# Reordering the 64 KB blocks of keys and values over the partitions in a single-token attention kernel

## The chip, the cores and the metric

The kernel runs on one core of one Trainium2 chip. The core has a matrix engine (PE, with a row of its own, PEld, for loading weights), a vector engine (DVE), a scalar engine (ACT), a general engine (POOL) and a sequencer that here only starts transfers (SP). 16 DMA engines move data between the chip's main memory and an on-chip memory of 128 partitions. The metric is the device time of one execution in microseconds (us). Before the change the median of three runs is 1275.43 us (1275.26 to 1275.6).

## The reference

One token goes through a layer norm, an attention over cached keys and values, and a small dense block; both have a residual.

```
H, Sk, Dh = 32, 32768, 128        # heads, cached positions, head size; D = 512, F = 1376
q = (layernorm(x) @ wq)                                      # one row of 32 x 128
scores = einsum("bhqd,bhkd->bhqk", q, k_cache) * Dh**-0.5
o = einsum("bhqk,bhkd->bhqd", softmax(scores), v_cache)
h = x + o @ wo
out = h + mish(layernorm(h) @ w1 + b1) @ w2
```

All tensors are bf16. The two caches have 32 heads of 32768 positions of 128 numbers each: 8 MB of keys and 8 MB of values a head, 537 MB in all. Each number is read once. The softmax and the weighted sum run over all positions of a head, in whatever order they stand, as long as keys and values stand in the same one.

## The kernel before

The on-chip memory holds a ring of six slots (`ring`), each of 32 KB a partition. A head's keys fill two slots, its values two: 64 KB a partition, 256 rows of 128 numbers (`SCOLS` = 256). Keys have two homes, for even and odd heads; values have one. `keys_of` (line 505) views a head's cache as `(p r) d -> p r d`: partition p takes the p-th of 128 blocks of 64 KB, that is positions 256 p to 256 p + 255. `tiles_of` (line 502) views the two slots in the same shape.

SP starts all large transfers, in the order written out in `order`: the query weights, keys of head 0, then for each head h from 1 on keys of h and values of h - 1, and at the end the output weights, the last values and the dense block's weights. The loop over `order` in `program` waits, before each transfer, for the work that frees its slots (`freed_by`, `done_with`; line 553), and then starts it (line 584 for keys and values). All go through `start`, so the profile names their issues, and the waits before them, by line 545. Most heads' keys and values come in one transfer of 8 MB each; the first keys, the last values and a few others are cut along r by `pieces`, so that work can begin or end on a part. Values of head h are started once the product of head h - 1 with its values is done; keys of head h once the keys of head h - 2 have been transposed.

For each head PE transposes the 256 tiles of 128 x 128 keys in groups of eight (line 685), DVE copies each group out of the accumulator (`ering`, line 691), and PE multiplies the group by the query, one column of scores a tile (line 661). DVE takes the maximum (line 725), two small matrix products spread it (lines 731 and 736), ACT takes the exponential of all scores with its sum (line 741), and PE multiplies the 256 tiles of values by the weights into one column (line 712). Column r of the scores and tile r of the values belong to the same positions, because keys and values are laid out alike. The product with the values of a head runs after the transposes of the next head's keys. PE and DVE run these rounds as loops; the head number is a register.

After the last head come the output projection, the second layer norm and the dense block, whose weights are loaded at the very end: `w1` in four transfers of 344 KB, `w2` in three transfers of 128 partitions and one of the last 96 rows (line 545 again in the profile).

Of the kernel before, what the change touches and what calls it, by code (L numbers as in the profile page):

```python
# [307 lines left out]
def build_kernel(nc, A_x, A_k_cache, A_v_cache, A_wq, A_wo, B_w1, B_b1, B_w2, out):  # L308
# [16 lines left out]
    SCOLS = HALVES * TPS  # L325
# [103 lines left out]
    def pieces(what):  # L429
        kind, h = what  # L430
        if what in (("k", 0), ("v", H - 1)):
            at = CUTS[kind]
        else:
            at = [TPS] if what in (("k", 1), ("v", 1)) else [64] if what == ("k", H - 1) else []
        return list(zip([0] + at, at + [SCOLS]))
# [4 lines left out]
    def uncut(what):  # L440


        kind, h = what
        for r in CUTS[kind]:
            if not cut_at(kind, h, r) and (h == 0 or cut_at(kind, h - 1, r)):
                n = 1
                while h + n < H and not cut_at(kind, h + n, r):
                    n += 1
                yield r, n

    def later_k(h):

        if h == 2:
            for r in CUTS["k"]:
                yield r, sum(1 for n in range(1, H) if n == 1 or not cut_at("k", n, r))
# [17 lines left out]
    def slot_of(what):  # L473
        if what in HOMES:
            return HOMES[what]
        if what[0] in ("w1", "w2"):
            return HOMES[WL]
        return V_HOME if what[0] == "v" else what[1] % 2 * HALVES
# [14 lines left out]
    def freed_by(what):  # L493
        if what == WO:
            return done_with("k", H - 2, 0, SCOLS)
        if what[0] == "k" and what[1] > 1:
            return done_with("k", what[1] - 2, 0, SCOLS)
        if what == ("v", 0):
            return [free_name(WQ)]
        return []  # L500

    def tiles_of(what):
        return ring[:, slot_of(what):slot_of(what) + HALVES, :].rearrange("p s (r d) -> p (s r) d", d=Dh)

    def keys_of(cache, h):
        return cache[0, h, :, :].rearrange("(p r) d -> p r d", r=SCOLS)

    wq_v = ring[:, slot_of(("wq",)), :].rearrange("p (k n) -> p k n", k=KC)
    wo_v = ring[:, slot_of(("wo",)), :].rearrange("p (j n) -> p j n", j=32)
# [6 lines left out]
    def done_with(kind, h, r0, r1):  # L516
        if kind == "v":
            return [f"pv{h}_{r1}" if r1 in V_EVENTS else f"pv{h}"]
        return [free_name(("k", h, half)) for half in range(HALVES) if r0 < (half + 1) * TPS and r1 > half * TPS]
# [15 lines left out]
    def program(S):  # L535
# [8 lines left out]
        def start(dst, src, s):  # L544
            S.dma(SP, lambda: sp.dma_start(dst, src).then_inc(s, 16))  # L545
# [3 lines left out]
        for what in order:  # L549
            slot = slot_of(what)  # L550
            if what == ("k", 1):
                S.stay(SP)
            S.wait(SP, freed_by(what))
            flat = ring[:, slot, :]
            if what[0] == "wq":
                S.wait(SP, ["b1z"])
                start(b1r[0:FJ // 2, :], B_b1[0:FJ * 128].rearrange("(i p) -> i p", i=FJ // 2), s_b1)
                start(b1r[FJ // 2:FJ // 2 + 1, 0:FLAST], B_b1[FJ * 128:F].rearrange("(o p) -> o p", o=1), s_b1)
            elif what[0] == "wo":
                start(flat, A_wo.rearrange("(p j) n -> p (j n)", j=32), ready[slot])  # L560
            elif what == WL:
                start(wol_v, A_wo[(H - 1) * Dh:H * Dh, :], s_wl)
            elif what[0] == "w1":
                k = what[1]
                start(w1_v[:, k, :], B_w1[k * 128:(k + 1) * 128, :], w1_sems[k])
            elif what[0] == "w2":
                n = what[1]
                if n + 1 < len(W2_J):
                    j0, j1 = W2_J[n], W2_J[n + 1]
                    start(w2_v[:, j0:j1, :].rearrange("p (i s) n -> p i (s n)", s=2),  # L570
                          B_w2[j0 * 128:j1 * 128, :].rearrange("(i p s) n -> p i (s n)", p=128, s=2), w2_sems[n])
                else:
                    start(w2_v[0:FLAST, FJ, :], B_w2[FJ * 128:F, :], w2_sems[n])
            else:
                kind, h = what
                rows = keys_of(A_k_cache if kind == "k" else A_v_cache, h)
                for r0, r1 in pieces(what):
                    if kind == "v" and h:
                        S.wait(SP, done_with(kind, h - 1, r0, r1))
                    if what == ("k", 1):  # L580
                        s = ready[slot] if r0 else s_k1
                    else:
                        s = cut_sems[kind][r0] if r0 else ready[slot]
                    start(tiles_of(what)[:, r0:r1, :], rows[:, r0:r1, :], s)


                for r, n in uncut(what) if kind == "v" else later_k(h):
                    S.dma(SP, lambda r=r, n=n: sp.sem_inc(cut_sems[kind][r], 16 * n))
# [277 lines left out]
    log = {}  # L866
    counted = _Sched(nc, False, events, sems, log)
    program(counted)
    nc.sync.dma_start(ring[:, slot_of(WQ), :], A_wq.rearrange("(p k) n -> p (k n)", k=KC)).then_inc(ready[slot_of(WQ)], 16)
    with nc.Block() as block:  # L870
        for eng_name, attr in ((POOL, "gpsimd"), (SP, "sync"), (DVE, "vector"), (ACT, "scalar"), (PE, "tensor")):
            emitter = _Sched(nc, True, events, sems, log, only=eng_name)

            def _run(eng, emitter=emitter):
                program(emitter)
            getattr(block, attr)(_run)
            assert emitter.cnt == counted.cnt
# [31 lines left out]
```

## Time and profile before

| what | value |
|---|---|
| median of the runs | 1275.43 us |
| span of the profiled execution | 1273.6 us |
| from the span to the median | 1.8 us |
| PE busy | 1016.5 us (80%) |
| DVE busy | 715.8 us (56%) |
| bytes moved | 548.35 MB, 431 GB/s over the span |
| packets of 8 KB or more | 12350 - 2998 = 9352 |
| PE's longest wait in total | 204.9 us, 30 times, for keys (line 685) |

The span goes from the first to the last instruction of one execution taken by the hardware profiler. A window row gives, for a stretch of that span, the busy time of each engine with its instructions in brackets, the granted clock of PE as a share, the mean busy share of the 16 DMA engines and what they moved in GB/s. In some windows the share comes out slightly above 1. The chain of waits is followed back from the last instruction: at each step to what released it. A transfer's line gives its size, the number of such transfers, and the median time from issue to landing.

### The profile page before, as it was taken

How to read it: one execution, taken by the hardware profiler on the slowest of the kernel's cores; microseconds unless marked ns; L12 is line 12 of the kernel's file. 1: busy time of each engine (PE TensorE's matmuls, PEld its weight loads, DVE VectorE, ACT ScalarE, POOL GpSimd, SP SyncE). 2: the span in 40 equal slices, each digit the busy share in tenths (PEclk: the TensorE clock that was granted, in tenths of full speed). 3: DMA queues.
4: the chain of work that ended last, by engine and by line, in shares of the span. 5: the costliest groups of instructions: out<-in, count | busy, mean ns of one | idle time of the engine just before them, and what ended most of it. 6: DMA issues, size and time to landing. Idle time of an engine off the chain costs nothing.

```text
span 1273.6 us, 54445 instructions
## 1 busy us (share of the span) xinstructions
PE 1016.5 (80%) x25046; PEld 988.9 (78%) x25046; DVE 715.8 (56%) x1252; ACT 20.6 (2%) x71; POOL 0.9 (0%) x8
## 2 busy tenths in 40 slices
PE   4689877779777789777788777797777897777995
PEld 4689877779777789777788777797777887777994
DVE  2566664456654466644466644566544666445661
ACT  0000000000000000000000000000000000000000
POOL 0000000000000000000000000000000000000000
PEclk9888876778877688867788776787777887677885
DMA  9999999999999999999999999999999999999998
GB/s 403 445 417 437 432 438 434 440 428 428 432 438 430 445 428 428 430 440 428 445 430 428 430 438 430 440 434 428 428 438 432 434 440 428 428 436 434 426 435 353
DMA packets 12350, 548.35 MB, mean 431 GB/s; under 512 B 1360, under 2 KB 1590, under 8 KB 2998
## 3 DMA queue, kind: packets, MB, share of 16 engines
q1 hardware_dynamic: 12340, 548.22, 99.7%
q8 instruction: 8, 0.13, 0.0%
q10 hardware_dynamic: 2, 0.00, 0.0%
HBM read 548.21 MB, written 0.00 MB: 430 GB/s over the span
## 4 chain that ended last, share of the span: by engine, by line
DMA 54%; DVE 23%; PE 18%; issue 2%; SPq 2%; POOL 0%; POOLq 0%
DMA ring<-in_A_k_cache_dram 51%; DVE ering L691 23%; PE ops L712 9%; PE tps L685 6%; DMA ring<-in_A_v_cache_dram 2%; SPq L545 2%; PE sps L661 1%; DMA ring<-in_B_w_dram 1%; PE hlp L736 1%; PE hlp L731 1%; PE hlp L746 0%; PE tps L854 0%; DVE pmax L725 0%; DVE perm L859 0%; DVE gmax L733 0%
## 5 line engine op out<-in xcount | busy, mean ns | idle before, releaser
L685 PE MATMUL tps<-identb,ring 128*128 128x128 bf16 x8192 | 668.3, 232 | 209.4 <-DMA ring<-in_A_k_cache_dram 204.9
L691 DVE COPY ering<-tps 128x1024 bf16<-128x1024 bf16 x1024 | 669.4, 692 | 259.7 <-PE tps L685 258.5
L685 PEld LDWEIGHTS tps<-identb,ring 128*128 x8192 | 522.2, 104 | 212.2 <-issue 212.2
L661 PE MATMUL sps<-qcur,ering 128*128 128x1 bf16 x8192 | 343.7, 164 | 7.7 <-DVE ering L691 6.7
L661 PEld LDWEIGHTS sps<-qcur,ering 128*128 128x128 bf16 x8192 | 309.2, 97 | 10.7 <-DVE ering L691 9.4
L712 PEld LDWEIGHTS ops<-pbuf,ring 128*128 128x128 bf16 x8192 | 226.3, 103 | 24.4 <-issue 15.1
L712 PE MATMUL ops<-pbuf,ring 128*128 128x1 bf16 x8192 | 231.3, 165 | 10.8 <-DMA ring<-in_A_v_cache_dram 8.3
L720 DVE TENSOR_TENSOR oT<-ops,rtotc 128x1 f32 x31 | 5.0, 162 | 109.8 <-PE ops L712 109.8
L733 DVE TENSOR_REDUCE gmax<-hlp 1x1 f32<-1x128 f32 x32 | 8.9, 278 | 67.5 <-PE hlp L731 67.5
L738 DVE TENSOR_SCALAR nbias<-hlp 128x1 f32<-128x1 f32 x32 | 5.1, 158 | 63.4 <-PE hlp L736 63.4
L741 ACT ACTIVATE pbuf<-sps,nbias 128x256 bf16<-128x256 f32 x32 | 15.2, 474 | 1219.9 <-PE ops L712 1166.7
L731 PE MATMUL hlp<-ident,pmax 128*1 128x128 f32 x64 | 17.9, 379 | 5.2 <-issue 5.2
L725 DVE TENSOR_REDUCE pmax<-sps 128x1 f32<-128x256 f32 x32 | 13.6, 425 | 14.3 <-PE sps L661 14.3
L736 PE MATMUL hlp<-gmax,onesmat 1*128 1x1 f32 x64 | 18.5, 356 | 0.4 <-DVE gmax L733 0.4
L736 PEld LDWEIGHTS hlp<-gmax,onesmat 1*128 1x128 f32 x64 | 15.8, 304 | 1.3 <-DVE gmax L733 0.9
L746 PE MATMUL hlp<-esum,onesmat 128*128 128x1 f32 x64 | 12.1, 258 | 4.8 <-issue 1.0
L746 PEld LDWEIGHTS hlp<-esum,onesmat 128*128 128x128 f32 x64 | 9.5, 188 | 7.4 <-issue 7.4
L640 PE MATMUL hlp<-xnT,ring 128*128 128x1 bf16 x128 | 3.6, 165 | 9.2 <-DMA ring<-in_A_wq_dram 9.2
L640 PEld LDWEIGHTS hlp<-xnT,ring 128*128 128x128 bf16 x128 | 3.5, 104 | 9.3 <-issue 9.3
L720 DVE TENSOR_TENSOR oL<-ops,rtotc 128x1 bf16<-128x1 f32 x1 | 0.2, 161 | 14.3 <-PE ops L712 14.3
L731 PEld LDWEIGHTS hlp<-ident,pmax 128*1 128x1 f32 x64 | 2.8, 81 | 5.8 <-issue 5.3
L748 DVE RECIPROCAL rtotc<-hlp 128x1 f32<-128x1 f32 x32 | 5.4, 168 | 2.7 <-PE hlp L746 1.4
(77 smaller groups left out, 40.1 us busy)
## 6 DMA issues: line engine op xcount, KB each, us to landing
ring<-in_A_k_cache_dram SPq DMA_DIRECT2D x3, 4096.0 KB, 40.2
ring<-in_A_v_cache_dram SPq DMA_DIRECT2D x3, 4096.0 KB, 15.3
ring<-in_A_k_cache_dram SPq DMA_DIRECT2D x3, 2048.0 KB, 30.5
ring<-in_A_k_cache_dram SPq DMA_DIRECT2D x1, 6144.0 KB, 44.6
ring<-in_A_wq_dram SPq DMA_DIRECT2D x1, 4096.0 KB, 12.2
ring<-in_A_wo_dram SPq DMA_DIRECT2D x1, 4096.0 KB, 35.6
ring<-in_A_v_cache_dram SPq DMA_DIRECT2D x1, 2048.0 KB, 16.1
ring<-in_B_w_dram SPq DMA_DIRECT2D x4, 344.0 KB, 20.7
```

The lines of the kernel that those rows point to most:

```text
L545: S.dma(SP, lambda: sp.dma_start(dst, src).then_inc(s, 16))
L640: S.step(PE, lambda h=h, kc=kc: t_.matmul(Q_REG[:, h:h + 1], wq_v[:, kc, h * Dh:(h + 1) * Dh], xnT[:, 0, kc:kc + 1], start=(kc == 0), stop ...
L661: S.step(PE, lambda r=r: t_.matmul(S_ps[:, col0 + r:col0 + r + 1], ering[:, bg % NE, r, :], qcur[:, :], start=True, stop=True), name=(name ...
L685: S.step(PE, lambda r=r, at=at: t_.matmul(tb[:, r * 128:(r + 1) * 128], key_tile(S, at), identb[:, :], is_transpose=True, start=True, stop ...
L691: S.step(DVE, lambda: v.tensor_copy(ering[:, bg % NE, :, :].rearrange("p r d -> p (r d)"), tb[:, :]), name=f"ev{bg}", waits=[f"trb{bg}"], ...
L712: S.step(PE, lambda r=r: t_.matmul(o_ps[:, 0:1], vt[:, r, :], pbuf[:, r:r + 1], start=(r == 0), stop=(r == SCOLS - 1)), name=(names or Non ...
L725: S.step(DVE, lambda: v.tensor_reduce(pmax[:, :], S_ps[:, 0:SCOLS], AXX, ALU.max), name=f"pmax{h}", waits=[f"qkh{h}"], kind="pmax")
L731: S.step(PE, lambda: t_.matmul(A_REG, pmax[:, :], ident[:, :], start=True, stop=True), name=f"A{h}", waits=[f"pmax{h}", "ident", f"rcp{h - ...
L733: S.step(DVE, lambda: v.tensor_reduce(gmax[:, :], A_REG, AXX, ALU.max), name=f"gmax{h}", waits=[f"A{h}"], kind="gmax")
L736: S.step(PE, lambda: t_.matmul(B_REG, onesm[0:1, :], gmax[:, :], start=True, stop=True), name=f"B{h}", waits=[f"gmax{h}", "consts0"] + ([] ...
L741: S.step(ACT, lambda: a.activation(pbuf[:, :], S_ps[:, 0:SCOLS], ACTF.Exp, bias=nb[:, :], scale=SC, accum_out=esum[:, :]), name=f"exp{h}", ...
L746: S.step(PE, lambda: t_.matmul(C_REG, onesm[:, :], esum[:, :], start=True, stop=True), name=f"C{h}", waits=[f"exp{h}"], kind="C")
```

## The change

Every load of keys and of values takes another order of the head's 64 KB blocks. Where partition 8 e + i (e from 0 to 15, i from 0 to 7) had block 8 e + i, it now has block 16 i + e. `keys_of` gives a view of four dimensions, (16, 8, 256, 128), and the start of a transfer folds the last two on the source's side, and the rows of the tile on the destination's: the source then counts 16 by 8 runs, the destination 128 partitions, each run as long as before. Cuts along r are as before.

```diff
     def keys_of(cache, h):
-        return cache[0, h, :, :].rearrange("(p r) d -> p r d", r=SCOLS)
+        return cache[0, h, :, :].rearrange("(i e r) d -> e i r d", e=16, r=SCOLS)
...
-                    start(tiles_of(what)[:, r0:r1, :], rows[:, r0:r1, :], s)
+                    start(tiles_of(what)[:, r0:r1, :].rearrange("p r d -> p (r d)"),
+                          rows[:, :, r0:r1, :].rearrange("e i r d -> e i (r d)"), s)
```

Keys and values go through the same function, so both are permuted alike.

## The prediction

> **What bounds the kernel now.** I read the page first, then the stages in windows, the chain of waits, the wait list of the SP queue, and last the end of the run in small windows. From the page: the engines' busy time, the share of the DMA engines by slice, the queue, and the chain that ended last.
>
> ```profile
> span 1273.6 us, 54445 instructions
> PE 1016.5 (80%) x25046; PEld 988.9 (78%) x25046; DVE 715.8 (56%) x1252; ACT 20.6 (2%) x71; POOL 0.9 (0%) x8
> DMA  9999999999999999999999999999999999999998
> DMA packets 12350, 548.35 MB, mean 431 GB/s; under 512 B 1360, under 2 KB 1590, under 8 KB 2998
> q1 hardware_dynamic: 12340, 548.22, 99.7%
> DMA 54%; DVE 23%; PE 18%; issue 2%; SPq 2%; POOL 0%; POOLq 0%
> ```
>
> One queue, filled by SP, carries all the bytes, and its packets take 99.7% of the time of 16 engines. No compute engine is full. The windows over five stages of the steady part say whether the rate wanders (columns: busy time of each engine, granted clock, DMA share, GB/s):
>
> ```profile
> core 0: us, PE busy (x) PEld busy (x) DVE busy (x) ACT busy (x) POOL busy (x), PEclk, DMA share, GB/s
> 200.00:400.00 200.00, 157.19 (x3911) 153.63 (x3907) 111.02 (x191) 3.39 (x12) 0.00 (x0) 0.76 1.01 435
> 400.00:600.00 200.00, 159.92 (x3926) 156.36 (x3927) 113.36 (x194) 2.83 (x10) 0.00 (x0) 0.76 1.00 432
> 600.00:800.00 200.00, 161.29 (x4023) 157.66 (x4020) 116.43 (x200) 2.83 (x10) 0.00 (x0) 0.77 1.00 433
> 800.00:1000.00 200.00, 163.23 (x4024) 159.80 (x4023) 117.24 (x200) 2.83 (x10) 0.00 (x0) 0.77 1.00 435
> 1000.00:1200.00 200.00, 163.15 (x4057) 159.75 (x4055) 117.68 (x203) 2.82 (x10) 0.00 (x0) 0.78 1.00 433
> ```
>
> 432 to 435 GB/s in every stage: the pace is that of a fixed link. Two rows of the chain of waits in order of time, each the first transposes after a head's keys have come, give it exactly, with the wait before the first of them and the two lines of loads of a whole head:
>
> ```profile
> 201.54 45.43 DMA ring<-in_A_k_cache_dram
> 247.37 3.59 PE tps L685 x32
> ...
> 1021.44 3.59 PE tps L685 x32
> ```
>
> ```profile
> ring<-in_A_v_cache_dram SPq DMA_DIRECT2D x30, 26.1
> ring<-in_A_k_cache_dram SPq DMA_DIRECT2D x29, 45.0
> ```
>
> Between them lie 774.07 us and 20 heads (the starts repeat every 77.4 us, for two heads): 38.70 us a head. A head is 8 MB of keys and 8 MB of values, 256 blocks of 64 KB, 16 for each engine if they share evenly: 2.42 us a block, 433.5 GB/s. The 32 heads are 32 x 38.70 = 1238 us of the 1273.6; the rest is the start, the weights and the end. A value load takes 26.1 us from issue to landing, and half of a head, 19.35 us, is its own transfer, so 6.7 us of other loads are still queued when it is issued.
>
> **The change part by part.** The arithmetic is untouched: keys and values are permuted alike, and neither the maximum, the sum nor the weighted sum over all positions asks for their order. Instructions on PE, DVE and ACT stay as they are. Bytes stay. The number and length of contiguous runs stay too: a partition still takes one whole 64 KB block of a head, or the same cut of it. Three things differ.
>
> (1) *SP's issues.* The source of each load gets one more dimension. The wait list of the SP queue and its timeline (rows of start, length, instruction):
>
> ```profile
> SPq L545 <- PE ops L712: 1165.8, 33, 38.8
> ```
>
> ```profile
> 1207.62 0.33 SPq L545 DMA_DIRECT2D ring<-in_A_v_cache_dram  x1
> 1208.05 0.38 SPq L545 DMA_DIRECT2D ring<-in_A_wo_dram  x1
> ```
>
> An issue holds SP for 0.33 to 0.38 us, and SP waits 1165.8 us for PE. Dearer issues vanish in that wait. Only the five pieces of the last head's values are issued with the end near; were each issue twice as long, 5 x 0.38 = 1.9 us would be the most. I take 0, bounds 0 to +1.9 us. Behind that wait stand the value load and the next key load; the 6.7 us of queue cover them.
>
> (2) *The order of reading.* Now an engine walks blocks 1 MB apart, and the 16 engines together walk 16 neighbouring blocks, where before each had neighbours of its own. A gain would need a pace above that of the fixed link: the best 200 us window has 435 for the 433.5 of the sum, and 1238 x (1 - 433.5/435) = 4.3 us is the most to be had. A loss: the slowest stretch of steady loading is early,
>
> ```profile
> 64.00:103.00 39.00, 35.32 (x882) 34.52 (x880) 26.22 (x45) 0.56 (x2) 0.00 (x0) 0.82 0.98 421
> ```
>
> 421 for 433.5, which over all heads would be 1238 x 0.030 = +37 us. Between -4.3 and +37 I take 0, by the five rows in which five different sets of heads give one rate.
>
> [...]
>
> (3) *How a load is divided among the engines.* This decides. Before, both sides count 128 rows. After, the source counts 16 times 8 and the destination 128, so an engine's sixteenth should be one value of e: partitions 8e to 8e + 7, walked in order. If that is not the share the engines had, two of them may now write into the same part of the on-chip memory at the same time, and the even pace rests on their not doing so. No load of the trace has unlike counts on its two sides. The nearest one is the only large one that isn't 128 rows, the last 96 rows of w2 (96 KB), at the very end:
>
> ```profile
> ring<-in_B_w_dram SPq DMA_DIRECT2D x1, 96.0 KB, 10.0
> ```
>
> ```profile
> 1267.50:1268.00 0.50, 0.50 (x9) 0.50 (x6) 0.22 (x1) 0.00 (x0) 0.00 (x0) 0.50 1.04 381
> 1268.00:1268.50 0.50, 0.38 (x2) 0.08 (x1) 0.18 (x3) 0.21 (x1) 0.00 (x0) 0.50 0.99 358
> 1268.50:1268.80 0.30, 0.00 (x0) 0.00 (x0) 0.27 (x2) 0.00 (x0) 0.00 (x0) 0.50 0.80 215
> 1268.80:1269.10 0.30, 0.00 (x0) 0.00 (x0) 0.27 (x2) 0.00 (x0) 0.20 (x1) 0.50 0.48 171
> 1269.40:1269.90 0.50, 0.50 (x16) 0.30 (x16) 0.00 (x0) 0.00 (x0) 0.00 (x0) 0.50 0.45 170
> ```
>
> Divide GB/s by the share: 366, 362, 269, 356, 378. For 0.3 us the busy engines move 0.74 of their bytes, and then recover: packets are stretched while loads divided in two ways overlap. What stretches them is not shown; two writers on one entry would do it. The last row says more: near 0.45 of the engines are still busy 1.4 us after the others (from 1268.5 to 1269.9), so engines lead one another by about 1.4 us at most.
>
> [...]
>
> The price, from rows: if no two engines meet, 0. If two always meet, each block takes 2 x 2.42 us, a head 77.4 us, and 32 heads 1238 us more. Compute doesn't limit then: PE's 163 us of 200 is 32 us a head. A lead helps: an engine that is 1.4 us ahead leaves the shared entry earlier. Four blocks are 9.68 us; met all the way they take 19.35, with the lead 19.35 - 1.4 = 17.95, a factor of 1.855. Between 1.855 and 2 I take 1.93. Of the two ends, nothing and twice, I take the upper: the row of stretched packets is the only one in which loads are divided in unlike ways. It is a choice on thin ground.
>
> *Sum.* The profiled execution: 1273.6 + 0 + 0 + 0.93 x 1238 = 2425 us. The median of the runs, 1275.4, is 1.8 us above the span, which I add: **2427 us**. With factors of 1.855 and 2, 2334 to 2514.
>
> **The rivals.**
>
> *No two engines meet, or the shares are what they were.* Then the fixed link goes on setting the pace: 1275.4, from 1273 to 1278. For it: five stages at one rate, whatever is loaded. Against it: the stretched row. This one ends on the other side, not slower, and it decides as soon as the 16 engines still write to 16 separate entries.
>
> *They meet, but drift apart.* [...] The lead now is 1.4 us; if it grows on the way, the loads end anywhere between 1 and 1.85 times as long. With the stretch of the row, 362/269 = 1.35, it is 1275.4 + 0.35 x 1238 = 1709 us. Against it: a load's end is its slowest engine's, and an engine that runs ahead soon waits for SP, which waits for PE, and starts level again.
>
> [...]
>
> *Neighbouring blocks read better:* at most -4.3 us, 1271 us. Against it: the DMA share is full and the rate flat, so reading is not what is waited for.
>
> That the change does nothing at all is out, since the addresses differ by construction.
>
> **How the numbers follow.** Two engines on one entry throughout (2334 to 2514): 0.45. Meeting and drifting (1310 to 2334): 0.17. Memory (1278 to 1312, and beyond by the page): 0.06. No difference: 0.24. Reading better: 0.08. A measurement of this kernel tells about 0.2%, 2.6 us, from no change. So slower 0.45 + 0.17 + 0.06 = 0.68, same 0.24, faster 0.08. The time is that of the likeliest, 2427 us, its own range 2334 to 2514. The range for 8 in 10 has to take in the no-difference case, since leaving it and the gain out would drop 0.32; it goes from 1272, most of the gain left out, to 2515, the full doubling.
>
> **What would show it.** In the changed profile: if right, the DMA share stays near 99% while GB/s falls to 220 to 235, a head takes 72 to 77 us, PE falls to some 45% busy, and value loads take over 45 us to land. SP's wait for PE must not be what grows first. A rate above 400 GB/s with the time within 3 us of before would make the third step wrong: the shares, or the entries, are not what limits. A rate between, changing along the run, would be drift. A small loss with an even rate would be the memory, and a gain of over 4.3 us would mean that the link is not fixed.

## The result and the profile after

The changed kernel takes 2610.63 us (median of six runs, 2603.67 to 2620.92), the kernel before 1275.39 us: a ratio of 2.0476, 95% interval 2.0448 to 2.0503. The profiled execution has a span of 2606.8 us and a time of 2608.6 us.

The lines of the page after the change that answer to those shown of before: engines, share of the DMA engines, packets, the queue.

```profile
span 2606.8 us, 54445 instructions
PE 1034.0 (40%) x25046; PEld 1003.8 (39%) x25046; DVE 716.6 (27%) x1252; ACT 20.6 (1%) x71; POOL 1.0 (0%) x8
DMA  9999999999999999999999999999999999999987
DMA packets 12350, 548.35 MB, mean 210 GB/s; under 512 B 1360, under 2 KB 1590, under 8 KB 2998
q1 hardware_dynamic: 12340, 548.22, 99.1%
```

The same instructions, the same 12350 packets, the same bytes, and still a busy share of 99.1% over all 16 engines: each packet lasts about twice as long (a 64 KB block 4.987 us on the mean, before 2.422). PE's busy time has hardly moved (1016.5 to 1034.0 us); only its share has fallen. That is the trap of a busy share: 99% is what a queue shows at 431 GB/s and at 210.

Windows of the steady part, with the columns of before (the last two are DMA share and GB/s):

```profile
400.00:800.00 400.00, 157.83 (x3870) 153.79 (x3870) 110.98 (x190) 2.83 (x10) 0.00 (x0) 0.63 1.00 211
1200.00:1600.00 400.00, 158.43 (x3870) 154.38 (x3870) 110.97 (x190) 2.83 (x10) 0.00 (x0) 0.63 1.00 211
2000.00:2400.00 400.00, 156.55 (x3870) 152.51 (x3870) 110.37 (x190) 2.82 (x10) 0.00 (x0) 0.63 1.01 212
```

An even 211 GB/s from end to end: no drift along the run. The chain of waits in order of time gives the pace; the rows are the wait for keys after a head's values have been used, 22 heads apart:

```profile
542.32 31.88 another core or an unknown queue
...
2306.24 31.84 another core or an unknown queue
```

The chain does not name what these waits are for ("an unknown queue"); the list of waits does. First the two lines of before, then those after:

```profile
PE tps L685 <- DMA ring<-in_A_k_cache_dram: 204.9, 30, 7.9
PE ops L712 <- DMA ring<-in_A_v_cache_dram: 8.3, 6, 4.0
```

```profile
PE tps L686 <- DMA ring<-in_A_k_cache_dram: 986.4, 34, 36.8
PE ops L713 <- DMA ring<-in_A_v_cache_dram: 530.7, 36, 29.2
```

1763.92 us for 22 heads are 80.18 us a head, where it was 38.70: a factor of 2.072. PE now waits for keys 986.4 us instead of 204.9, and for values 530.7 us instead of 8.3. The lines of the whole loads, from issue to landing:

```profile
ring<-in_A_v_cache_dram SPq DMA_DIRECT2D x30, 71.9
ring<-in_A_k_cache_dram SPq DMA_DIRECT2D x29, 111.4
```

71.9 us for a value load (26.1 before). Half a head is now 40.1 us, so 31.8 us of other loads are queued at the issue instead of 6.7: SP is further ahead than before, and is not what is late.

### The profile page after: what moved, and what is told of

Same layout as the page of the kernel before. It is cut to its first block, busy times and chain, and to the rows that moved or that the text cites. A ratio compares the mean times of both kernels' runs of the same rounds, so it can differ in the third digit from the quotient of the medians.

```text
span 2606.8 us, 54445 instructions
## 1 busy us (share of the span) xinstructions
PE 1034.0 (40%) x25046; PEld 1003.8 (39%) x25046; DVE 716.6 (27%) x1252; ACT 20.6 (1%) x71; POOL 1.0 (0%) x8
## 2 busy tenths in 40 slices
DMA packets 12350, 548.35 MB, mean 210 GB/s; under 512 B 1360, under 2 KB 1590, under 8 KB 2998
## 3 DMA queue, kind: packets, MB, share of 16 engines
q1 hardware_dynamic: 12340, 548.22, 99.1%
## 4 chain that ended last, share of the span: by engine, by line
another core or an unknown queue 56%; DVE 21%; PE 18%; DMA 3%; issue 2%; SPq 0%; POOL 0%; ACT 0%; POOLq 0%
DVE ering L692 21%; PE ops L713 9%; PE tps L686 6%; DMA ring<-in_A_k_cache_dram 2%; DMA ring<-in_B_w_dram 2%; PE sps L662 1%; PE hlp L732 1%; PE hlp L737 1%; PE hlp L747 0%; SPq L545 0%; PE tps L855 0%; PE sps L835 0%; DVE pmax L726 0%; DVE perm L860 0%
## 5 line engine op out<-in xcount | busy, mean ns | idle before, releaser
L686 PE MATMUL tps<-identb,ring 128*128 128x128 bf16 x8192 | 678.2, 234 | 990.7 <-DMA ring<-in_A_k_cache_dram 986.4
L686 PEld LDWEIGHTS tps<-identb,ring 128*128 x8192 | 530.0, 105 | 993.5 <-issue 993.5
L713 PE MATMUL ops<-pbuf,ring 128*128 128x1 bf16 x8192 | 234.1, 165 | 535.9 <-DMA ring<-in_A_v_cache_dram 530.7
L742 ACT ACTIVATION_READ_ACCUMULATOR pbuf<-sps,nbias 128x1 f32 x32 | 6.2, 193 | 0.0
```

Of the source, the lines that this page charges most:

```text
L686: S.step(PE, lambda r=r, at=at: t_.matmul(tb[:, r * 128:(r + 1) * 128], key_tile(S, at), identb[:, :], is_transpose=True, start=True, stop ...
L713: S.step(PE, lambda r=r: t_.matmul(o_ps[:, 0:1], vt[:, r, :], pbuf[:, r:r + 1], start=(r == 0), stop=(r == SCOLS - 1)), name=(names or Non ...
L742: S.step(ACT, lambda: a.activation(pbuf[:, :], S_ps[:, 0:SCOLS], ACTF.Exp, bias=nb[:, :], scale=SC, accum_out=esum[:, :]), name=f"exp{h}", ...
```

## The experiments

Two things change at once: the order in which blocks are read, and the counts on the two sides of a load (16 by 8 against 128). The first theory, of division, is my supposition that unlike counts give each engine other partitions, and that two engines then write into one part of the on-chip memory at one time, which prediction and expectations call an entry. No record of these runs shows an entry, which partitions an engine wrote, or which blocks were read at one time: where the texts say how many entries a set of partitions reaches, or which blocks an engine has, that is supposed too. The rival says that the order of reading slows the memory. Unless said otherwise, an edit touches all loads of keys and values. Of longer edits the lines of the loads are shown, with ... where others are left out. The loads with 8 KB runs (e10) were run four times and those with 32 by 4 (e11) ten times, every other variant once; single runs are read for large differences alone.

**Unlike counts, almost the old order (e1_unlike_near).**

```diff
-        return cache[0, h, :, :].rearrange("(i e r) d -> e i r d", e=16, r=SCOLS)
+        flat = cache[0, h, :, :]
+        return bass.AP(flat.tensor, flat.offset, [[8 * SCOLS * Dh - Dh, 16], [SCOLS * Dh, 8], [Dh, SCOLS], [1, Dh]])
```

> The source counts 16 by 8 as in the changed kernel, but its blocks lie almost as before: block 8 e + i, moved back by e rows of 256 bytes, so that a few positions are read twice and the last ones are left out. Division theory (a load with unlike counts gives each engine 8 neighbouring partitions, and two engines write into one entry): as slow as the changed kernel, 2550 to 2650 us, about 210 GB/s. Reading-order theory (1 MB steps of an engine, or neighbouring blocks at one time, slow the memory): 1275 us, 431 GB/s.

Measured: 2600.98 us. Its page:

```profile
DMA packets 12350, 548.35 MB, mean 211 GB/s; under 512 B 1360, under 2 KB 1590, under 8 KB 2998
q1 hardware_dynamic: 12340, 548.22, 99.8%
```

Nearly the old addresses, and the full loss. The order of reading is not needed for it.

**Like counts, the new steps (e2_like_steps).**

```diff
-        return cache[0, h, :, :].rearrange("(p r) d -> p r d", r=SCOLS)
+        if 2 <= h <= H - 2:
+            return cache[0, h, :, :].rearrange("(s p r) d -> p s (r d)", s=8, p=128)
...
-                    start(tiles_of(what)[:, r0:r1, :], rows[:, r0:r1, :], s)
+                    if 2 <= h <= H - 2:
+                        start(tiles_of(what).rearrange("p (s r) d -> p s (r d)", s=8), rows, s)
+                    else:
+                        start(tiles_of(what)[:, r0:r1, :], rows[:, r0:r1, :], s)
```

> Both sides count 128 again, and each partition takes 8 runs of 8 KB that lie 1 MB apart, in the loads of heads 2 to 30. Division theory: the division is that of before, so 1275 us, up to 1320 if the shorter packets cost something. Reading-order theory by the 1 MB steps: near 2610 us, or at least some hundred us above 1275.

Measured: 1306.3 us. **The same runs without the steps (e10_runs_8k)** says where its 31 us are from:

```diff
-        def start(dst, src, s):
-            S.dma(SP, lambda: sp.dma_start(dst, src).then_inc(s, 16))
+        def start(dst, src, s, **m):
+            S.dma(SP, lambda: sp.dma_start(dst, src, **m).then_inc(s, 16))
...
-                    start(tiles_of(what)[:, r0:r1, :], rows[:, r0:r1, :], s)
+                    start(tiles_of(what)[:, r0:r1, :], rows[:, r0:r1, :], s, **(dict(max_dma_last_dim=8192) if 2 <= h <= H - 2 else {}))
```

> Blocks, counts and order as before, but the loads of heads 2 to 30 are cut into runs of 8 KB. The kernel with 8 KB runs 1 MB apart took 1306 us. If its 31 us came from the shorter packets: 1300 to 1310 us here. If they came from the 1 MB steps: 1275 to 1280 us.

Measured: 1306.02 us, ratio 1.0239 (1.0222 to 1.0256). The packet lines, first of the loads with steps, then of those without:

```profile
DMA packets 64318, 548.35 MB, mean 420 GB/s; under 512 B 1360, under 2 KB 1590, under 8 KB 2998
```

```profile
DMA packets 64318, 548.35 MB, mean 420 GB/s; under 512 B 1360, under 2 KB 1590, under 8 KB 2998
```

The lines are equal to the last digit and the times 0.3 us apart: the 1 MB steps cost nothing that one run can show, the 51,968 packets more cost 31 us. With e1 the 1 MB steps have fallen from both sides. The other half of the rival, neighbouring blocks read at one time, is answered by e6 and e11 below.

**Neighbouring partitions with like counts (e3_halves, e8_quarters, e5_sixteens).** Blocks and counts as before, but each load is two, four or eight loads of 64, 32 or 16 neighbouring partitions; semaphore counts are scaled to match.

```diff
...
-                    start(tiles_of(what)[:, r0:r1, :], rows[:, r0:r1, :], s)
+                    for part in range(2):
+                        ps_ = slice(64 * part, 64 * part + 64)
+                        start(tiles_of(what)[ps_, r0:r1, :], rows[ps_, r0:r1, :], s)
```

> Blocks and counts as before, but each load of keys or values is two loads of 64 neighbouring partitions. Division theory: 64 neighbours reach half of the entries, so two engines share one all the time: 2550 to 2700 us. Reading-order theory, and the theory that only unlike counts are slow: 1275 to 1290 us.

> Blocks and counts as before, each load in four, of 32 neighbouring partitions. [...] If an entry were 8 neighbours, 32 would reach 4 entries, four engines each: 5000 us and more.

> Blocks and counts as before, each load in eight, of 16 neighbouring partitions. They reach 4 entries, so four engines share one: twice the time of two on one, 4600 to 5300 us. If the loss of the halves and quarters were a cost of each extra load instead (two or four loads gave the same time), eight would give about 2600 us.

Measured: 2609.95, 2611.35 and 4733.22 us. The packet and queue lines, of halves, quarters and sixteens:

```profile
DMA packets 13520, 548.37 MB, mean 210 GB/s; under 512 B 2528, under 2 KB 2758, under 8 KB 4166
q1 hardware_dynamic: 13508, 548.22, 99.7%
```

```profile
DMA packets 15856, 548.38 MB, mean 210 GB/s; under 512 B 4864, under 2 KB 5094, under 8 KB 6502
q1 hardware_dynamic: 15844, 548.23, 100.0%
```

```profile
DMA packets 20530, 548.42 MB, mean 116 GB/s; under 512 B 9536, under 2 KB 9766, under 8 KB 11174
q1 hardware_dynamic: 20516, 548.25, 100.2%
```

All 16 engines are busy in each (99.7, 100.0 and 100.2%). With like counts and the old blocks, a load confined to 64 neighbouring partitions is as slow as the changed kernel, and 32 are no slower than 64: 210 GB/s each, where 5000 us and more had been put down for 32 if an entry were eight neighbours. With 16 the rate nearly halves again, to 116 GB/s. That engines share entries would fit these three times; the times themselves show that loads confined to neighbouring partitions are slow, near half the rate of before (431 GB/s) at 64 and 32 and near a quarter at 16. Each of these loads also reads from a narrower stretch of memory, 4, 2 and 1 MB. That is hardly what slows them: in e2 the runs of one step lie in 1 MB, as far as the engines keep step, and with 32 by 4 (below) neighbouring blocks would be read at one time, by its counts, and these two kept 420 and 431 GB/s.

**64 partitions spread out (e4_odd_even).** As e3_halves, with `slice(part, 128, 2)` in place of the slice of neighbours.

> Blocks and counts as before, but each load is two, of the even and of the odd partitions. Together the 64 partitions of each reach every entry; an engine's share would be four of 8 neighbours, in order. Division theory with engines that meet: 2500 to 2650 us, as in the changed kernel. If it is enough that a load as a whole reaches all entries, or if only unlike counts or the reading order are slow: 1275 to 1290 us.

Measured: 1276.19 us; the packet line of e3_halves with another rate:

```profile
DMA packets 13520, 548.37 MB, mean 430 GB/s; under 512 B 2528, under 2 KB 2758, under 8 KB 4166
```

This missed what I had put down for the division theory. As many loads, packets and semaphores as with halves, and the full rate: 430 GB/s for 210. So it is not how many partitions a load covers that slows it, but which. If the theory holds, the engines are not given neighbouring rows in order in these loads; how the 64 rows are dealt out was not shown. "An engine's sixteenth" had to be put more finely.

**The same spread with unlike counts (e9_unlike_odd_even)**, that is the changed kernel with each load in two:

```diff
...
-                    start(tiles_of(what)[:, r0:r1, :].rearrange("p r d -> p (r d)"),
-                          rows[:, :, r0:r1, :].rearrange("e i r d -> e i (r d)"), s)
+                    for part in range(2):
+                        start(tiles_of(what)[part:128:2, r0:r1, :].rearrange("p r d -> p (r d)"),
+                              rows[:, part:8:2, r0:r1, :].rearrange("e i r d -> e i (r d)"), s)
```

> The changed kernel's order, each load in two, of the even and of the odd partitions: source 16 by 4, destination 64. The same split with like counts took 1276 us. If unlike counts alone set the division, engine e still has four of 8 neighbours: 2500 to 2650 us. If the split into even and odd partitions is what spreads the engines: 1276 to 1290 us.

Measured: 2491.71 us. Against e4_odd_even the source differs, 16 by 4 blocks in the new order, and the way the rows are folded, which e6 and e11 share without loss. With 16 outermost the full rate is gone: 220 GB/s for 430.

**Unlike counts with more outside (e6_unlike_64x2, e11_unlike_32x4).** The changed kernel with another factor:

```diff
-        return cache[0, h, :, :].rearrange("(i e r) d -> e i r d", e=16, r=SCOLS)
+        return cache[0, h, :, :].rearrange("(i e r) d -> e i r d", e=64, r=SCOLS)
```

> The source counts 64 by 2, the destination 128: partition 2 e + i takes block 64 i + e, so an engine's steps are 64 KB and 4 MB instead of 1 MB. If any unlike counts give an engine 8 neighbouring partitions: 2550 to 2650 us, like the changed kernel. If the counts 16 by 8 or the 1 MB steps are special: 1275 us.

> The source counts 32 by 4, the destination 128: partition 4 e + i takes block 32 i + e, so an engine's steps are 2 MB and neighbouring blocks are read at the same time. [...]

Measured: 1275.43 us with 64 by 2, which missed the division theory's number; and 1275.42 us with 32 by 4, for which 1275 and 2500 to 2650 us had both been put down, a ratio of 1.0 (0.9991 to 1.001). The page of the latter:

```profile
span 1273.6 us, 54445 instructions
q1 hardware_dynamic: 12340, 548.22, 99.7%
```

So "unlike counts" is not the condition either. For loads of 128 partitions, 128, 64 and 32 outermost are fast (1275.43, 1275.43 and 1275.42 us), 16 is slow (2610.63 us). Why 32 outermost keep the pace and 16 lose it was not shown, and neither was why 64 rows lose it as neighbours (2609.95 us) and keep it as every second one (1276.19 us): which partitions an engine wrote is not in any record. So what decides the dealing stays open.

The packet records show the loss block by block. These are mean durations in ns of the first 32 KB blocks of keys, 16 at a time in the order in which they started (one round of the engines); in the kernel before, such a block takes 1213 ns:

```
changed kernel       2372 2564 2564 2548 2377 2562 2553 2532
e9_unlike_odd_even   2344 2559 2345 2556 2334 2558 2358 2541
e8_quarters          2328 2568 2552 2538 2354 2560 2562 2531
e3_halves            2369 2562 2564 2550 2381 2560 2568 2554
```

In the changed kernel, the quarters and the halves one round in four is shorter, by 179 to 240 ns against the round after it; in e9 it is one in two, by 183 to 224 ns. I take a short round for one in which the engines come to another entry, which in e9 would happen twice as often; that is an estimate from these patterns, and what makes a round short was not shown.

**The new order in values alone (e7_values_only).**

```diff
-                    start(tiles_of(what)[:, r0:r1, :], rows[:, r0:r1, :], s)
+                    if kind == "v":
+                        start(tiles_of(what)[:, r0:r1, :].rearrange("p r d -> p (r d)"),
+                              rows.rearrange("(i e) r d -> e i r d", e=16)[:, :, r0:r1, :].rearrange("e i r d -> e i (r d)"), s)
+                    else:
+                        start(tiles_of(what)[:, r0:r1, :], rows[:, r0:r1, :], s)
```

> The new order in the loads of values alone; the values are then weighted with other positions' weights. Division theory: the value half of each head takes twice its time and the key half its old time, so half of the loss: 1275 + (2609 - 1275) / 2 = 1942 us, from 1900 to 1980. If the slow loads disturb the ones beside them, or if the engines drift apart in the fast loads: off this by over 100 us, above or below.

Measured: 2139.16 us, 197 above the sum: half of the loads carry (2139 - 1275) / (2611 - 1275) = 65% of the loss. The queue line, and windows of 20 us:

```profile
q1 hardware_dynamic: 12340, 548.22, 93.4%
```

```profile
1000.00:1020.00 20.00, 8.20 (x260) 7.64 (x260) 0.60 (x3) 0.56 (x2) 0.00 (x0) 0.50 0.78 226
1020.00:1040.00 20.00, 6.72 (x108) 6.73 (x109) 4.90 (x8) 0.00 (x0) 0.00 (x0) 0.56 1.01 210
1060.00:1080.00 20.00, 7.31 (x233) 6.84 (x234) 0.43 (x2) 0.00 (x0) 0.00 (x0) 0.50 0.76 315
1080.00:1100.00 20.00, 0.88 (x34) 0.80 (x30) 0.16 (x1) 0.56 (x2) 0.00 (x0) 0.50 1.01 213
```

Here the busy share does fall: in some stretches nearly a quarter of the engines' time is idle, at 226 GB/s in the first. The packet records show who is idle there: at 1008 and at 1010 us two of the 16 engines have a packet under way and 14 have none. SP issues the next loads only after that:

```profile
1012.72 0.54 SPq L545 DMA_DIRECT2D ring<-in_A_v_cache_dram  x1
1013.36 0.53 SPq L545 DMA_DIRECT2D ring<-in_A_k_cache_dram  x1
```

So engines that come first through a mixed sequence of loads have nothing queued, while the load is not done until the two late ones are: PE's wait for these keys ends only at 1032.88. Why they come apart so far when the two kinds alternate, and not when all loads are of one kind, was not tried. What does not hold is that half of the loads carry half of the loss.

No variant beat the kernel before. The block order that was meant, neighbouring blocks at one time, is in e6_unlike_64x2 and e11_unlike_32x4, and gains nothing.

## Why the prediction was right or wrong

*What bounds the kernel:* right. Transfers set the end before and after; PE's busy time of 1034 us disappears in waits.

*SP's issues at nothing:* right. 32 by 4 has a source of as many dimensions and 1275.42 us.

*Order of reading at nothing:* right, shown by e1 one way and by e6, e11 and e2 beside e10 the other. With steps of 1 MB inside a partition and without them, the two kernels of 8 KB runs are 0.3 us apart. The chances allowed the memory a loss beyond 1312 us: no run shows a ground for that, and what the runs showed in its place is these 0.3 us.

*The division of a load:* the runs bear out the loss, and that it hangs on which partitions a load writes and with what counts (64 neighbours at 210 GB/s, 64 spread out at 430; 16 outermost at 210, 32 at 431). That engines meet on shared entries was my estimate, and no run shows it. Its ground in the trace was thin, so that taking the upper end was in part luck. Packets of one size do stretch beside the 96-row load: by the packet records of before, those of 2 KB that start between 1268.5 and 1268.75 us take 122 ns on the mean, those of the quarter microsecond from 1267.75 on 88. Whether they stretched at a shared entry was not tried. What the text put down as its condition, unlike counts, was too wide. e6 and e11 have unlike counts and are fast (1275.43 and 1275.42 us); in loads of 128 partitions 16 outermost is what does it.

*The step that failed is the price,* "Between 1.855 and 2 I take 1.93", and with it the end of the range at "the full doubling". Measured is 2.072 a head: 32 x (80.18 - 38.70) = 1327 us in place of 0.93 x 1238 = 1151; the rest of the span went from 35 to 41 us. Two things were wrong in it.

First, a doubling is no upper bound. A 64 KB block takes 2.422 us before, 4.987 us in the changed kernel and 5.021 in halves: 2.06 and 2.07 times. Taken 16 at a time as above, the 64 KB blocks of the changed kernel settle into fours like 4758, 5099, 5116 and 4980 ns, and those of halves into 4847, 5120, 5121 and 5004. The long ones are 2.11 times the block of before: if two engines meet there all the way, sharing costs more than half the rate.

Second, the lead was mis-sized. That it counts once in four blocks, 9.68 us, is a term that no run shows; what the runs showed is one short round in four, and a small gain from it. Against four blocks of 5116 ns, the four of the changed kernel save 0.5 us, not the 1.4 us that were read from the end of the run. Only where one round in two is short (e9) is the gain larger, 4.780 us a block and 2491.71 us in all.

The signs say the same. The busy share (99.1%) and the landing of value loads (71.9 us, forecast over 45) came as forecast. The rate (211 GB/s for 220 to 235), the head (80.18 us for 72 to 77) and PE's share (40% for some 45%) all miss on the slow side.

*The rivals:* no drift (211 GB/s in windows from 400 to 2400 us), no memory, no gain. "No difference" is what 64 by 2 and 32 by 4 show, and no row that the prediction used told 16 from 32. The chances gave "slower" 0.68 on a row of 0.3 us.

## What to carry to other kernels

A reordering that is free in arithmetic and bytes can still halve the rate of the loads: 431 GB/s became 210 here, at busy shares of 99.7 and 99.1%. When a load's outermost counts change, look at GB/s, not at the busy share. If the order of blocks is to change, keep at least 32 outermost on the source's side of a load to 128 partitions, as 32, 64 and 128 were fast here (1275.42 to 1275.43 us); 16 outermost doubled the time (2610.63 us). No other count was tried on a load of 128 partitions. Where the rate was flat at one pace (432 to 435 GB/s), another order of reading won nothing (1275.42 and 1275.43 us for 1275.43).

## What the runs showed of the hardware

The loss does not grow evenly as a load is confined to fewer neighbouring partitions. A 64 KB block takes 2.422 us on the mean in the kernel before, 5.021 us in loads of 64 neighbours (halves), 2.07 times as long, and 9.231 us in loads of 16 (sixteens), 3.81 times; loads of 64 and of 32 run at one rate, 210 GB/s. If two engines share an entry in the halves and four in the sixteens, which no record shows, then one engine alone moves 65536 / 2.422 = 27.1 GB/s through an entry, two together 26.1, and four 4 x 65536 / 9.231 = 28.4: an estimate from these three durations. And 64 of 128 partitions are no limit by themselves: the even and odd ones load at 430 GB/s, neighbouring ones at 210.
